# Softmax denominators inverted before a shared transpose, two steps of q on other engines, and a new order of an attention stage

## The chip, the core and the metric

One core of a Trainium2 chip runs the whole program. The metric is the time of one execution on the device in microseconds, from the first to the last work of the core. Its engines work side by side, each through its own list of instructions in order: TensorE (PE, matmuls and transposes), VectorE (DVE), ScalarE (ACT), GpSimd (POOL) and SyncE (SP, which here only issues DMA transfers). An instruction that waits for a semaphore holds everything behind it on its engine.

## What is computed

Three layers in a row: an attention with rotary positions, a feed-forward layer with a squared ReLU, and a layer of 8 experts of which each token takes one. The change lies in the first one.

```python
q_rot, k_rot = (rotate(q), rotate(k))                 # 4 batches, 8 heads, 576 positions, 64 wide
scores = scale * np.matmul(q_rot, k_rot.transpose(0, 1, 3, 2))
scores = scores - np.max(scores, axis=-1, keepdims=True)
attn = np.exp(scores)
attn = attn / (np.sum(attn, axis=-1, keepdims=True) + 1e-09)
attn_out = np.matmul(attn, v)                         # float32
x = attn_out.transpose(0, 2, 1, 3).reshape(2304, 512)
x = np.maximum(x @ w_in, 0.0) ** 2 @ w_out            # moe
return experts(x)                                     # moe2: gate, argmax, w1, relu, w2
```

## The kernel before

**Pairs.** The 32 heads are worked in 16 pairs, numbered 0 to 15. Each pair goes through steps that have short names; a name with a pair's number (pair 9's trm03) is one step of one pair. Numbers in float32 are kept as a high part in the form that PE reads (fp32r) and a low part, the remainder; a copy makes the high part, a subtraction the low one.

- ldk, ldq, ldv load k, q and v of a pair (SP). ak, bk, ck and aq, bq, cq turn k and q (two products with tables and a sum, L184, L186).
- kh0, kh1, kl0, kl1 split the two heads of k (copies L168 or L170, subtractions L173); kd0, kd1 copy the high part to the other 64 lanes. qh0, qh1, ql0, ql1 do the same for q: the digit is the head. vhi and vlo split v.
- sc0 to sc8 are nine tiles of scores (L238), 128 queries by 576 keys; sc8 holds the last 64 queries of both heads and takes twice the matmuls. mx0 to mx8 take the negated row maximum on DVE (L245), ex0 to ex8 the exponential on ACT (L256), which also sums each row into a column of a 128x9 tile.
- tr... transposes e on PE in tiles of 128x512 (L295): trm00 to trm13 for the main blocks (head, block), trrk and trrq for the remainders over keys and over queries, and trrr for the 64x64 corner of both remainders. eh... copies each to SBUF on ACT, el... subtracts the remainder on DVE (L173).
- srec adds 1e-9 to the sums and inverts them. In the kernel before it works on the transposed sums, 9 lanes of 128, in PSUM: trrr makes two transposes into one PSUM tile (L285, L286), ehrr and elrr read one half and srec (L265, L266) the other. rst stores the 9x128 result to memory; for block 0 (pairs 0 to 3) rld reads it back over 64 lanes and xn multiplies, later blocks are normalized in the next stage.
- pv00 to pv11 multiply with v (L329), p1.. copies the result to the tile xo (ACT), p2.. adds the two halves for pairs 0 to 3; xh and xl split the normalized result there, xr and xst store it.

**Rings.** Scores stand in a ring of two PSUM tiles, transposes and products in a ring of four called b, so a transpose waits until the tile four places back was read out. raw, vs, et0, et1, rk and xo have one buffer, the halves of q and k two, by the pair's parity; e and its sums have two tiles of the pool a_sb.

**Order.** The order is written out by hand as numbers: `FIRST`, `SECOND` and `PLAN` (from line 40) give each step a time and an engine (T for PE, A for ACT, V for DVE, P for POOL, D for a DMA on SP), for pair 0, pair 1 and all others; pair p is shifted by p x PERIOD (18), and all steps are recorded in the order of these numbers. The numbers only sort. So each engine's list interleaves two to four pairs. `TAIL` mixes in the first steps of the feed-forward layer: w.. steps convert int64 weights to float32 (wd loads one, wx on ACT, wy on DVE, wz on POOL, wb on DVE, wh on ACT, wl on POOL), xs0 to xs3 load the tokens of block 0, cl seven small constants, setup works on those, m10 to m12 are first products, re, sq, gg and gl the squared ReLU in two parts, m20 a second product. The unnamed step of the plan ("open") closes the pool a_prep, whose memory the feed-forward layer then takes.

Of the kernel before, what the change touches and what calls it, by code (L numbers as in the profile page):

```python
# [34 lines left out]
def f32(ap):  # L35
# [28 lines left out]
}  # L64
FIRST = {
# [25 lines left out]
}  # L91
SECOND = {
# [51 lines left out]
def attention(tc, qx, kx, v, tabq, tabk, ident, eye, xT, rD, ps, tail=None):  # L144
    nc = tc.nc
# [1093 lines left out]
```

## Time and profile before

| | us |
|---|---|
| median of 3 runs | 1060.05 (1059.29 to 1061.39) |
| the profiled execution | 1060.22 |
| its span, first to last instruction | 1058.4 |
| PE busy in the span | 942.7 |
| DVE | 740.3 |
| ACT | 543.3 |
| POOL | 391.7 |

Times in the views are microseconds from the span's start. The attention ends at 369 us with the last copy of pair 15; the conversion of the weights goes on to about 480 us, and from there TensorE works nearly without a gap. A row of a timeline gives the start, the duration, the engine, the line and the operation, the tile written and those read; in brackets stands how long the engine was idle before, and what ended that. A window gives each engine's busy time in a stretch and the clock that was granted to TensorE, as a share of 2.4 GHz: 0.5 is the lower level, 1.2 GHz.

### The profile page before, as it was taken

The page shows a single profiled execution, that of the slowest core. Times are in us where ns is not written, and L with a number is a line of the kernel's source. Part 1 is how long each engine was busy: PE and PEld are TensorE (multiplying, and loading weights), DVE is VectorE, ACT ScalarE, POOL GpSimd, SP SyncE. Part 2 cuts the span into 40 slices and gives each one's busy share as a digit, 9 for nine tenths or more (in the row PEclk, how much of TensorE's full clock was granted, in tenths as well). Part 3 has the DMA queues.
Part 4 walks back from the last instruction along what each step waited for, and adds up shares of the span by engine and source line. Part 5 has one row for each costly group of instructions (what it writes and reads, how often), then busy time and mean ns, then how long its engine had stood idle before and what let it go on. Part 6 is the DMA issues. An engine that isn't in the chain of part 4 may idle for free. (4 is left out here: it accounts for less than half of the span.)

```text
span 1058.4 us, 14903 instructions
## 1 busy us (share of the span) xinstructions
PE 942.7 (89%) x5194; PEld 817.8 (77%) x5194; DVE 740.3 (70%) x1298; ACT 543.3 (51%) x1089; POOL 391.7 (37%) x277
## 2 busy tenths in 40 slices
PE   2778888988988868878999999999999999999996
PEld 1667777887887846656887888788898889999995
DVE  5898878888888689997765575376456476566660
ACT  3677777887887746653223312321234325555551
POOL 7666676667664265564300220020001022212111
PEclk9899898999998989999999999999999999999998
DMA  6224344444443443543400310110015147766730
GB/s 235 92 87 138 116 121 145 130 139 134 129 137 81 129 141 120 170 138 131 155 5 1 119 41 1 60 41 1 1 41 180 40 159 222 237 214 224 241 121 31
DMA packets 50674, 122.90 MB, mean 116 GB/s; under 512 B 10960, under 2 KB 15584, under 8 KB 50592
## 3 DMA queue, kind: packets, MB, share of 16 engines
q1 hardware_dynamic: 47552, 112.17, 33.8%
q0 software_dynamic: 3040, 9.70, 2.6%
q8 instruction: 43, 0.70, 0.3%
q14 instruction: 39, 0.32, 0.1%
HBM read 98.23 MB, written 19.21 MB: 111 GB/s over the span
## 5 line engine op out<-in xcount | busy, mean ns | idle before, releaser
L658 PE MATMUL h<-xs,w 128*128 128x512 f32 (+1 forms) x720 | 169.6, 383 | 15.6 <-POOL w L511 15.6
L664 ACT ACTIVATE r<-h 128x512 f32<-128x512 f32 (+1 forms) x80 | 44.4, 555 | 237.5 <-PE h L658 194.8
L658 PEld LDWEIGHTS h<-xs,w 128*128 128x128 f32 x720 | 129.9, 194 | 46.9 <-POOL w L511 20.0
L672 DVE TENSOR_TENSOR g<-r 128x512 f32<-128x512 f32 (+1 forms) x80 | 65.1, 813 | 119.9 <-ACT r L664 119.1
L238 PE MATMUL sc<-kh,q 128*128 128x288 f32 x320 | 109.1, 356 | 40.4 <-DVE q L173 18.6
L295 PE MATMUL b<-ident,e 128*128 128x128 f32 x640 | 111.3, 316 | 34.5 <-DVE et L173 28.0
L693 PE MATMUL y<-w,gh 128*128 128x512 f32 x432 | 137.1, 399 | 0.0
L256 ACT ACTIVATE e<-sc,nmx 128x576 f32<-128x576 f32 x144 | 106.3, 740 | 50.2 <-DVE nmx L245 48.9
L245 DVE TENSOR_REDUCE nmx<-sc 128x1 f32<-128x576 f32 x144 | 105.7, 749 | 26.8 <-PE sc L238 25.5
L295 PEld LDWEIGHTS b<-ident,e 128*128 128x128 f32 x640 | 89.9, 163 | 43.8 <-DVE et L173 21.1
L238 PEld LDWEIGHTS sc<-kh,q 128*128 128x128 f32 x320 | 68.3, 214 | 50.4 <-issue 26.1
L930 DVE TENSOR_TENSOR w<-eraw,w 128x1024 fp32r<-128x1024 f32 x64 | 78.3, 1224 | 33.8 <-ACT w L929 33.7
L168 ACT ACTIVATE et<-b 128x512 fp32r<-128x512 f32 (+1 forms) x160 | 84.5, 550 | 25.4 <-PE b L295 24.7
L173 DVE TENSOR_TENSOR et<-b,et 128x512 fp32r<-128x512 f32 (+1 forms) x160 | 94.7, 623 | 4.0 <-ACT et L168 3.0
L238 PE MATMUL sc<-kl,q 128*128 128x288 f32 x320 | 96.9, 318 | 0.0
L693 PEld LDWEIGHTS y<-w,gh 128*128 128x128 f32 x432 | 81.3, 191 | 18.0
L693 PE MATMUL y<-w,gl 128*128 128x512 f32 x216 | 85.5, 396 | 0.0
L329 PE MATMUL b<-et,vs 128*128 128x288 f32 x512 | 80.7, 299 | 0.0
L975 PEld LDWEIGHTS h<-ye,w 128*128 128x128 f32 x576 | 75.1, 189 | 3.9
L975 PE MATMUL h<-ye,w 128*128 128x256 f32 x576 | 76.3, 283 | 0.0
L705 DVE SCALAR_TENSOR_TENSOR junk<-ysb,wgb 128x512 f32<-128x512 f32 x96 | 75.6, 841 | 0.0
L998 PE MATMUL y<-w,ge 128*128 128x512 f32 x288 | 75.3, 397 | 0.0
(218 smaller groups left out, 1836.5 us busy)
## 6 DMA issues: line engine op xcount, KB each, us to landing
eraw<-wexp SPq DMA_DIRECT2D x64, 512.0 KB, 3.6
wraw<-wio SPq DMA_DIRECT2D x32, 512.0 KB, 4.3
rawk<-kx SPq DMA_DIRECT2D x15, 640.0 KB, 3.9
rawq<-qx SPq DMA_DIRECT2D x15, 576.0 KB, 3.7
xT<-xo SPq DMA_DIRECT2D x24, 288.0 KB, 3.5
vraw<-v SPq DMA_DIRECT2D x16, 320.0 KB, 3.6
yD<-ysb SPq DMA_DIRECT2D x18, 256.0 KB, 2.0
kh<-kh SPq DMA_DIRECT2D x15, 160.0 KB, 2.4
```

Of the source, the lines that this page charges most:

```text
L168: nc.scalar.activation(out=out, in_=in_, func=ACTF.Copy)
L173: on[eng].tensor_tensor(out=out, in0=in0, in1=f32(hi), op=ALU.subtract)
L238: nc.tensor.matmul(out=sc(p, j)[:, half, 0:HS], lhsT=q[:, hd, q0:q0 + 128], rhs=k[:, hd, k0 + half * HS:k0 + half * HS + HS], start=(n == ...
L245: nc.vector.tensor_reduce(out=m, in_=sc(p, j)[:, :, 0:HS], axis=AX.XY, op=ALU.max, negate=True)
L256: nc.scalar.activation(out=e(p)[:, o:o + S].rearrange("p (a b) -> p a b", a=2), in_=sc(p, j)[:, :, 0:HS], func=ACTF.Exp, bias=live[p, f"nm ...
L295: nc.tensor.transpose(t[:, i * 128:(i + 1) * 128], x[:, o:o + 128], ident)
L329: nc.tensor.matmul(out=o, lhsT=lhsT.rearrange("p a b -> p (a b)"), rhs=rhs, start=(c == 0 and i == 0), stop=(c == 4 and i == 1))
L658: nc.tensor.matmul(out=h, lhsT=w[:, a, k * 128:(k + 1) * 128], rhs=xs[b, k][:, c], start=(k == 0 and i == 0), stop=(k == 3 and i == 2))
L693: nc.tensor.matmul(out=yp[t], lhsT=g[a][:, t * 128:(t + 1) * 128], rhs=w[:, c, 512:1024], start=(f == 0 and i == 0), stop=(f == NFC - 1 an ...
L705: nc.vector.scalar_tensor_tensor(out=junk, in0=ysb[j], scalar=1.0, in1=wgb[e], op0=ALU.mult, op1=ALU.mult, accum_out=lg[:, j, e:e + 1])
L930: nc.vector.tensor_tensor(out=w[:, 1], in0=r, in1=f32(w[:, 0]), op=ALU.subtract)
L975: nc.tensor.matmul(out=h, lhsT=w[:, a, k * 128:(k + 1) * 128], rhs=x[:, c], start=(k == 0 and i == 0), stop=(k == 3 and i == 2))
```

## The change

1. The sums lie behind e in the same tile (columns 9S to 9S+9, in 64 columns that are cleared once). e is no longer a tile of the pool a_sb, but one of two tiles of a_prep (e0, e1).
2. A new step sa adds 1e-9 to the 128x9 sums in place, on POOL. srec inverts them in place on DVE.
3. trrr is one transpose of the corner and the 64 columns behind it; the nine inverted sums come out in lanes 64 to 72 of the corner's tile. A new step sev copies them to rs on DVE.
4. In all pairs but pair 0, qh1 is ACT's and ql1 POOL's; both were DVE's. (Pair 0 keeps its engines.)
5. All four tables have new numbers.

```diff
 PLAN = {
-    "aq": (-96.168, "P"), ... "qh0": (-88.995, "V"), "qh1": (-88.827, "V"),
-    "ql0": (-87.629, "V"), ... "ql1": (-86.558, "V"), ...
+    "cq": (-76.464, "P"), "qh0": (-76.362, "V"), "qh1": (-74.157, "A"),
+    "ql0": (-73.664, "V"), "ql1": (-73.273, "P"), ...
+    ... "sa": (-45.720, "P"), ... "srec": (-44.605, "V"), ... "sev": (-42.856, "V"), ...
...
+        e_buf = [prep.tile([128, 9 * S + 64], F32, name=f"e{i}") for i in range(2)]
...
         def e(p):
-            return get(p, "e", [128, 9 * S], F32, 2)
+            return e_buf[p % 2]
 
         def sums(p):
-            return get(p, "sum", [128, 9], F32, 2)
+            return e(p)[:, 9 * S:9 * S + 9]
...
+        def guard(p, eng):
+            on[eng].tensor_scalar(out=sums(p), in0=sums(p), scalar1=1e-9, scalar2=None, op0=ALU.add)
+
         def srec(p, eng):
-            r = rs(p)
-            nc.vector.tensor_scalar(out=r, in0=tb(p, "rr")[0:9, 128:256], scalar1=1e-9, scalar2=None, op0=ALU.add)
-            nc.vector.reciprocal(out=r, in_=r)
+            nc.vector.reciprocal(out=sums(p), in_=sums(p))
+
+        def sev(p, eng):
+            copy(eng, rs(p), tb(p, "rr")[64:73, 0:128])
...
             if g == "rr":
-                nc.tensor.transpose(t[0:64, 0:128], x[:, 8 * S + 512:9 * S], ident)
-                nc.tensor.transpose(t[0:9, 128:256], sums(p), ident)
+                nc.tensor.transpose(t[:, 0:128], x[:, 8 * S + 512:9 * S + 64], ident)
                 return
...
+        for i in range(2):
+            nc.vector.memset(e_buf[i][:, 9 * S:9 * S + 64], 0.0)
```

The new numbers show in the engines' lists. Lines are those of each kernel. DVE, in the middle of the attention, around srec; et and rk are the transposed e, a number behind a name tells tiles apart; before:

```order
L173 TENSOR_TENSOR q_83<-rawq,q_83 64x576 x2
L173 TENSOR_TENSOR et_2465<-b,et_2465 128x512
L245 TENSOR_REDUCE nmx<-sc 128x1 x2
L265 TENSOR_SCALAR rs<-b 9x128
L266 RECIPROCAL rs<-rs 9x128
L173 TENSOR_TENSOR et_2465<-b,et_2465 128x512
L245 TENSOR_REDUCE nmx<-sc 128x1
L173 TENSOR_TENSOR et_2465<-b,et_2465 128x512
```

and now:

```order
L248 TENSOR_REDUCE nmx<-sc 128x1
L270 RECIPROCAL e_90<-e_90 128x9
L248 TENSOR_REDUCE nmx<-sc 128x1
L176 TENSOR_TENSOR et_2439<-b,et_2439 128x4x64
L176 TENSOR_TENSOR et_2514<-b,et_2514 128x4x64
L176 TENSOR_TENSOR rk<-b,rk 128x512
L173 COPY rs<-b 9x128
L248 TENSOR_REDUCE nmx<-sc 128x1
L176 TENSOR_TENSOR et_2439<-b,et_2439 128x512
L176 TENSOR_TENSOR rk<-b,rk 64x64 x2
L173 CAST q_84<-rawq 64x576
```

The two instructions of srec between the remainders (L265, L266) gave way to a short reciprocal between two maxima and a copy four rows on; one cast of q stands alone behind the remainders of the corner, with its subtraction further down.

POOL, one period; kl, vs and rawk, rawq are the low parts of k, v and the raw k and q, and L173 or L176 are subtractions; before:

```order
L186 TENSOR_TENSOR rawk<-rawk 128x640
L184 TENSOR_TENSOR rawq<-rawq,tabq 128x576 x2
L173 TENSOR_TENSOR kl_87<-rawk,kh_85 64x640
L173 TENSOR_TENSOR kl_87<-rawk,kh_85 64x576
L186 TENSOR_TENSOR rawq<-rawq 128x576
L173 TENSOR_TENSOR vs<-vraw,vs 128x10x64
L184 TENSOR_TENSOR rawk<-rawk,tabk 128x640 x2
L186 TENSOR_TENSOR rawk<-rawk 128x640
```

and now:

```order
L176 TENSOR_TENSOR q_83<-rawq,q_83 64x576
L187 TENSOR_TENSOR rawk<-rawk,tabk 128x640 x2
L189 TENSOR_TENSOR rawk<-rawk 128x640
L187 TENSOR_TENSOR rawq<-rawq,tabq 128x576
L267 TENSOR_SCALAR e_90<-e_90 128x9
L187 TENSOR_TENSOR rawq<-rawq,tabq 128x576
L176 TENSOR_TENSOR kl_88<-rawk,kh_86 64x640
L176 TENSOR_TENSOR kl_88<-rawk,kh_86 64x576
L189 TENSOR_TENSOR rawq<-rawq 128x576
L176 TENSOR_TENSOR vs<-vraw,vs 128x10x64
L176 TENSOR_TENSOR q_84<-rawq,q_84 64x576
```

The addition to the sums (L267) stands between the two products for q, the subtraction for v is followed by the one for q's second head, and only then does the next pair's k begin.

SP at the end of the attention; xT is the store of a pair's result, wraw the weights, c_, wg_sb, mb_sb and mod_sb the seven constants; before, where the four xs loads (L541) stand just ahead of the first row:

```order
L458 DMA wraw<-wio 128x512
L269 DMA rD<-rs 9x128
L356 DMA xT<-xo 64x2x576 x2
L600 DMA c_io_3901<-cst 128x8
L600 DMA c_io_3902<-cst 128x128
L600 DMA c_lt<-cst 128x128
L600 DMA c_id<-cst 128x18
L602 DMA wg_sb<-wg 128x4x8
L603 DMA mb_sb<-mb 128x16
L604 DMA mod_sb<-mod 128x18x2
L356 DMA xT<-xo 64x2x576 x2
L458 DMA wraw<-wio 128x512 x13
```

and now, from the xs loads on:

```order
L549 DMA xs<-xT 128x2x512 x4
L362 DMA xT<-xo 64x2x576 x2
L276 DMA rD<-rs 9x128
L362 DMA xT<-xo 64x2x576 x2
L608 DMA c_io_3872<-cst 128x8
L608 DMA c_io_3873<-cst 128x128
L608 DMA c_lt<-cst 128x128
L608 DMA c_id<-cst 128x18
L610 DMA wg_sb<-wg 128x4x8
L611 DMA mb_sb<-mb 128x16
L612 DMA mod_sb<-mod 128x18x2
L466 DMA wraw<-wio 128x512 x14
```

The constants stood ahead of the last xT stores and stand behind them now, with all further weights behind the constants. The xs loads stand ahead of the stores of pairs 14 and 15 in both; they go into memory that a_prep gave up, in which e0 and e1 lie now, and did not before.

## Rows read from the trace of the kernel before

**Rows 1.** Windows: busy us of PE, PEld, DVE, ACT, POOL; granted clock; DMA share, GB/s.
```profile
235.50:255.65 20.15, 17.68 (x124) 16.79 (x124) 16.33 (x29) 15.89 (x39) 13.21 (x10) 0.92 0.44 124
239.10:242.60 3.50, 1.46 (x11) 1.26 (x12) 3.46 (x7) 1.54 (x5) 3.42 (x3) 0.99 0.37 92
242.60:246.00 3.40, 3.40 (x18) 3.37 (x17) 3.37 (x7) 2.74 (x7) 1.81 (x2) 0.51 0.39 114
400.00:460.00 60.00, 49.68 (x188) 37.77 (x186) 58.43 (x69) 36.89 (x62) 36.97 (x24) 0.91 0.46 154
```

**Rows 2.** Timeline of POOL: start, us, what, idle before and releaser; vlo, and kl1.
```profile
38.17 1.63 POOL L173 TENSOR_TENSOR vs<-vraw,vs 128x640 fp32r<-128x640 f32 x1
...
85.85 1.84 POOL L173 TENSOR_TENSOR vs<-vraw,vs 128x640 fp32r<-128x640 f32 x1 [2.35 <-ACT vs L168]
...
175.14 1.56 POOL L173 TENSOR_TENSOR vs<-vraw,vs 128x640 fp32r<-128x640 f32 x1 [3.77 <-ACT vs L168]
...
235.50 1.55 POOL L173 TENSOR_TENSOR vs<-vraw,vs 128x640 fp32r<-128x640 f32 x1 [4.03 <-ACT vs L168]
...
246.46 1.57 POOL L173 TENSOR_TENSOR kl<-rawk,kh 64x640 fp32r<-64x640 f32 x1 [2.05 <-ACT kh L168]
...
334.77 1.57 POOL L173 TENSOR_TENSOR vs<-vraw,vs 128x640 fp32r<-128x640 f32 x1 [2.52 <-ACT vs L168]
```

**Rows 3.** Timeline of DVE: q of pair 1, then of pair 11, then srec.
```profile
36.25 2.16 DVE L170 CAST q<-rawq 64x576 fp32r<-64x576 f32 x2
...
39.11 3.07 DVE L173 TENSOR_TENSOR q<-rawq,q 64x576 fp32r<-64x576 f32 x2
...
252.43 0.93 DVE L170 CAST q<-rawq 64x576 fp32r<-64x576 f32 x2
253.39 1.54 DVE L173 TENSOR_TENSOR q<-rawq,q 64x576 fp32r<-64x576 f32 x2
...
258.75 0.28 DVE L265 TENSOR_SCALAR rs<-b 9x128 f32<-9x128 f32 x1 [1.66 <-ACT rk L168]
259.06 0.94 DVE L266 RECIPROCAL rs<-rs 9x128 f32<-9x128 f32 x1
```

**Rows 4.** Timeline of ACT: a cast of q in pair 0; an exponential.
```profile
14.68 0.68 ACT L168 ACTIVATE q<-rawq 64x576 fp32r<-64x576 f32 x1
...
241.09 0.74 ACT L256 ACTIVATE e<-sc,nmx 128x576 f32<-128x576 f32 x1 [1.91 <-DVE nmx L245]
```

**Rows 5.** Timeline of PE: transposes in a period and in the drain; second product.
```profile
240.44 0.66 PE L295 MATMUL b<-ident,e 128*128 128x128 f32 x4 [1.36 <-DVE et L173]
...
359.01 4.26 PE L295 MATMUL b<-ident,e 128*128 128x128 f32 x24 [2.56 <-DVE et L173]
...
384.86 1.22 PE L693 MATMUL y<-wf,gh 128*128 128x512 f32 x2 [7.63 <-ACT gh L668]
```

**Rows 6.** Groups of POOL, whole span: count, busy us and mean ns, idle before.
```profile
L885 POOL TENSOR_TENSOR rhs<-rhs,val 128x306 fp32r<-128x306 f32 x3 | 2.6, 884 | 47.9 <-DVE rhs L879 47.8
...
L173 POOL TENSOR_TENSOR q<-rawq,q 64x576 fp32r<-64x576 f32 x1 | 1.4, 1411 | 0.8 <-ACT q L168 0.8
...
L1216 POOL MEMSET const-uint8-127<- 128x1 uint8 x1 | 0.1, 119 | 0.0
```

**Rows 7.** Timeline of SP, the DMA queue, at the attention's end.
```profile
360.08 1.92 SPq L600 DMA_DIRECT2D c_io<-cst  x2
...
364.02 0.43 SPq L604 DMA_DIRECT2D mod_sb<-mod  x1
369.32 1.23 SPq L356 DMA_DIRECT2D xT<-xo  x2
370.65 47.98 SPq L458 DMA_DIRECT2D wraw<-wio  x12
```

**Rows 8.** DMA issues: count, KB each, median us from issue to landing.
```profile
wraw<-wio SPq DMA_DIRECT2D x32, 512.0 KB, 4.3
...
xT<-xo SPq DMA_DIRECT2D x24, 288.0 KB, 3.5
```

More of the change, by code (lines that the diff above doesn't have):

```diff
@@ L373, in xst @@
             nc.sync.dma_start(out=xT[p, :, :, 0:N0], in_=f32(xh(p)))
-        fs = dict(ldv=ldv, vhi=vhi, vlo=vlo, srec=srec, rst=rst, rld=rld, xr=xr, xn=xn, xh=xhi, xl=xlo, xst=xst)
+        fs = dict(ldv=ldv, vhi=vhi, vlo=vlo, sa=guard, srec=srec, sev=sev, rst=rst, rld=rld, xr=xr, xn=xn, xh=xhi, xl=xlo, xst=xst)
         for x in "qk":
```

190 rows, old and new, of tables (FIRST, PLAN, SECOND, TAIL) are left out of this document.

## Prediction

> **What bounds the kernel now.** I read the windows first. The attention runs to 369 us [rows 7]; behind it comes a stage in which DVE is busy 58.43 of 60 us, and then one filled by TensorE [rows 1]. All edits lie in the attention, or at its end. There no engine is full: in one period of 20.15 us PE is busy 17.68, DVE 16.33, ACT 15.89, POOL 13.21 [rows 1]. So the order binds, and the question is which waits make the loop.
>
> The start of vlo on POOL, one a pair, gives the pace: pairs 6 to 14 stand 159.63 us apart, 19.95 a pair; pairs 2 to 6, with extra work for block 0, 89.29, or 22.3; pairs 0 to 2, 47.7 [rows 2]. Within a period the loop is this. DVE comes to srec and waits 1.66 us, because L265 reads the PSUM tile that ACT is copying out of (ehrr); then it spends 0.28 and 0.94 on it [rows 3]. The maxima and remainders behind it come late: ACT idles 1.91 us for mx2 [rows 4] and PE 1.36 us for a tile of ring b [rows 5]. PE, busy 1.46 of 3.5 us there, then works at a granted clock of 0.51, the lower level, in the next 3.4 us [rows 1].
>
> **The change part by part.** *Denominators.* Out of DVE's queue go L265 (0.28) and the long reciprocal (0.94), and with them the wait of 1.66 [rows 3]. In come a reciprocal of 9 elements a lane and sev, a copy of the 9x128 shape of L265, so 0.28. The reciprocal took 0.94 for 128 elements a lane; for 9 it lies between nothing and 0.94, and I take 0.15, by element count. It waits for sa, the addition of 1e-9 on POOL. POOL's nearest rows are 0.12 us (one element a lane) and 0.88 (306) [rows 6]; I take 0.2, since 9 is near 1. One transpose less on PE is under 0.3 us in PE's slack. The wait does not vanish by itself: sev must wait for the shared transpose, and srec for sa; both are rivals below. In the order PE makes that transpose right behind sc1, and DVE has mx2, elrq and elrk (some 2 us) between srec and sev, which covers it.
>
> *q's second head.* qh1 goes from DVE (half of 0.93) to ACT (0.68 for the same shape in the first pair), ql1 from DVE (half of 1.54) to POOL (1.41) [rows 3, 4, 6]. Loads of a period then are: DVE 16.33 - 0.46 - 0.77 - 1.22 + 0.15 + 0.28 = 14.3; ACT 15.89 + 0.68 = 16.6; POOL 13.21 + 1.41 + 0.2 = 14.8. ACT is now the fullest, so a period is at least 16.6.
>
> *What remains of q on DVE.* Before, both casts and both subtractions stood where POOL idles (it waits 4.03 us for vhi), and cost 0.93 and 1.54. In the first pairs, with POOL at work, the same two pairs of instructions took 2.16 and 3.07 [rows 2, 3]. In the new order qh0 follows elrr, about a microsecond after vhi, when POOL has begun vlo; ql0 comes two maxima later, when POOL runs ql1. So each meets a POOL instruction. One cast costs 0 to 1.2 more, one subtraction 0 to 0.8; I take 0.5 (vlo is half done) and 0.7. Behind them stand mx8 and mx4, for which ACT waits, and ACT has no spare time: 1.2 us a period on the path. The Trainium skill says of this, in "GPSIMD Engine Reference", section Specifications, that GpSimd's SBUF interface is shared with VectorE and contended by DVE instructions with two SBUF inputs or in a two-port mode. By that rule taken in full it would be the rival B; the longer rows of the first pairs agree with it.
>
> *The order.* Period forecast: 16.6 + 1.2 + 0.2 for waits that I can't place (ACT idles 4.26 a period now) = 18.0, between 17.2 and 18.6. In a timetable by hand PE's thinnest stretch of 3.4 us holds four groups of transposes and a double score tile, about 2.5 us of work against 1.46 now, so I expect the granted clock to stay at the upper level. POOL: ak and aq wait for loads that start when kl0 and ql1 are done and land 4 us later; POOL has cq, vlo and ql1, or ak, bk and ck (over 4 us), in between, so no wait there.
>
> *The sum.* Nine steady periods (the eight of [rows 2] and the one with pair 15's scores): 9 x (19.95 - 18.0) = 17.6 less. Pairs 2 to 6: they stay 2.35 above a steady period, plus 0.45 because xn and xl meet a fuller POOL, so 20.8: 4 x 1.5 = 6 less (2 to 10). Front: half of the contended 2.16 and 3.07 goes from in front of pair 1's scores: 3 less (from 7 less to 2 more). Drain of pair 15: PE's 2.56 us wait behind srec stands uncovered [rows 5], and the transposes after it run slow: 3 less (1 to 4).
>
> *The handover costs.* Two things get worse at the attention's end. First, the seven loads of constants, 4.4 us of SP's time, ran beside the last transposes; they now stand behind the last xT store, and all weight loads from wd7 on behind them [rows 7]. Today the next weight load is issued at 370.65, right behind that store, and PE's second product starts at 384.86, 15.5 us behind the end of p110 [rows 5]. wd7 will be issued 1.3 + 4.4 behind it and land 4.3 later [rows 8]; wx7 then runs 4 us later than now. Second, e is now a tile of the pool that closes early, so the xs tiles of the next stage lie in its memory: their loads must wait for the last transpose of pair 15. The store of pair 14 stands behind them on SP, and p100 of pair 15 needs xo back from it: three issues, 1.3 us for the store, 3.5 to land [rows 8]; the p1 copies end some 3 us later. Together 7 more, between 2.5 (if DVE's own chain covers most of it) and 10.
>
> -17.6 - 6 - 3 - 3 + 7 = -22.6. The profiled execution took 1060.22 (span 1058.4), beside a median of 1060.05, so no correction: 1037.6, say 1038. The ends of the period and of the handover give 1024 to 1048.
>
> **The rivals.** *B, contention in full.* qh0 and ql0 wait out whole POOL instructions, 1.2 and 0.8, and POOL is held in turn: period 19.1. Then 9 x 0.85 = 7.7, and 2, 1 and 2 for pairs 2 to 6, front and drain, against 7: 6 less, 1054. For it: the rows of the first pairs [rows 3]. Against: POOL has 3 us of idle time a period in which they may fall. *C, sev takes the place of the wait.* If PE is late, DVE waits for the shared transpose as it did for ehrr; only the 0.94 is saved, and contention takes 1.2 of it back. Period 19.9 or so, drain and front 4 less, handover 4 to 7 more: 1060. Against: PE has more slack in the new order. *A, slower: sa holds DVE.* POOL works in order. If its waits stay as long as now (4.03 for vhi, 2.05 for kh [rows 2]), a POOL period is 14.8 + 6.1 = 20.9, plus the wait of sa for the last exponential, 0.5: 21.4 against 19.95. DVE stands at srec until sa is done, and all maxima behind it: 13 periods x 1.4 = 18 more, and 7 for the handover: 1085. It decides from 5.2 us of POOL waits a period (20.0 - 14.8); above that the kernel is slower. For it: POOL gets the two new steps and is in DVE's path for the first time. Against: vlo now has ql1 and the k of the next pair behind it, and the new places of kh0 and vhi on ACT match its order.
>
> **How the numbers follow.** Forecast 0.58, B 0.17, C 0.09, A 0.16. About 0.2% (2 us) is what a measurement can tell from no change. Faster: forecast and B, 0.75; same: C, 0.09; slower: A, 0.16. The range has to leave out no more than 0.2: it takes in the forecast's ends, B and C, up to 1063, and leaves A and a little below 1024.
>
> **What would show it.** Right: vlo starts 17.2 to 18.6 apart in pairs 6 to 14; DVE's wait ahead of sev and srec under 0.3 each; ACT busy over 90% of a period; the granted clock at the upper level in steady periods; qh0 about 0.9 and ql0 about 1.4; the second product 20 to 25 us behind the last p110. Wrong: the reciprocal waiting for POOL by more than 1 us (A), sev waiting for PE by as much (C), a clock that still falls once a period, or an early part that is longer than 47.7 and 89.3.

## The result, and the profile after

The changed kernel takes 1032.34 us (median of four runs, 1031.78 to 1033.71), the kernel before in the same comparison 1060.72: the ratio is 0.973, with a 95% interval of 0.970 to 0.976. The forecast was 1038 (1024 to 1063). The profiled execution of the changed kernel took 1031.78, with a span of 1030.0. So 28.4 us went out of the span, where 22.6 were forecast.

The windows of the changed kernel (start and end, length, then busy us of PE, PEld, DVE, ACT and POOL, the granted clock, DMA share and GB/s), first over pairs 6 to 14, then over one period; they answer to [rows 1]; the third row is the kernel before over the same pairs:

```profile
165.40:305.60 140.20, 133.26 (x972) 121.98 (x971) 123.73 (x209) 128.21 (x312) 112.46 (x82) 1.00 0.49 141
218.26:235.78 17.52, 16.65 (x123) 15.21 (x123) 15.44 (x27) 16.15 (x40) 15.41 (x11) 1.00 0.51 143
175.14:334.77 159.63, 139.79 (x974) 131.95 (x974) 132.92 (x226) 126.99 (x305) 107.04 (x73) 0.93 0.44 128
```

A period is 140.05/8 = 17.51 us, and the granted clock is 1.00 all through these eight, the upper level; before it was 0.93 over the same pairs, and fell to 0.51 in the period shown in [rows 1]. Now every engine is nearly full, and PE is the fullest: of 17.52 us PE is busy 16.65, ACT 16.15, DVE 15.44, POOL 15.41.

POOL's timeline (start, us, what, idle time before and its releaser): vlo of pairs 0, 2, 6, 9 and 14, as in [rows 2], and what follows it in pair 9's period:

```profile
38.38 1.95 POOL L176 TENSOR_TENSOR vs<-vraw,vs 128x640 fp32r<-128x640 f32 x1
...
93.64 1.55 POOL L176 TENSOR_TENSOR vs<-vraw,vs 128x640 fp32r<-128x640 f32 x1
...
165.71 1.55 POOL L176 TENSOR_TENSOR vs<-vraw,vs 128x640 fp32r<-128x640 f32 x1
...
218.29 1.55 POOL L176 TENSOR_TENSOR vs<-vraw,vs 128x640 fp32r<-128x640 f32 x1
220.69 1.42 POOL L176 TENSOR_TENSOR q<-rawq,q 64x576 fp32r<-64x576 f32 x1 [0.85 <-ACT q L171]
222.20 1.95 POOL L187 TENSOR_TENSOR rawk<-rawk,tabk 128x640 f32<-128x640 f32 x1
...
305.76 1.55 POOL L176 TENSOR_TENSOR vs<-vraw,vs 128x640 fp32r<-128x640 f32 x1 [4.53 <-ACT vs L171]
```

DVE's, one period, as in [rows 3]: qh0, ql0, srec (L270), mx2, and sev (L173 COPY):

```profile
219.36 0.79 DVE L173 CAST q<-rawq 64x576 fp32r<-64x576 f32 x1
...
221.45 1.28 DVE L176 TENSOR_TENSOR q<-rawq,q 64x576 fp32r<-64x576 f32 x1
...
231.49 0.20 DVE L270 RECIPROCAL e<-e 128x9 f32<-128x9 f32 x1
232.73 0.76 DVE L248 TENSOR_REDUCE nmx<-sc 128x1 f32<-128x576 f32 x1 [1.04 <-PE sc L241]
...
234.83 0.28 DVE L173 COPY rs<-b 9x128 f32<-9x128 f32 x1
```

ACT's: qh1, ex8, ex4 (with its accumulator read) and ex6 of that period, as in [rows 4]; ehrr (behind sev, which DVE starts at 234.83); then the last four p1 copies and the first step of wx7:

```profile
219.87 0.68 ACT L171 ACTIVATE q<-rawq 64x576 fp32r<-64x576 f32 x1
...
221.45 0.74 ACT L259 ACTIVATE e<-sc,nmx 128x576 f32<-128x576 f32 x1 [0.28 <-DVE nmx L248]
...
224.15 0.74 ACT L259 ACTIVATE e<-sc,nmx 128x576 f32<-128x576 f32 x1 [0.89 <-DVE nmx L248]
224.79 0.19 ACT L259 ACTIVATION_READ_ACCUMULATOR e<-sc,nmx 128x1 f32 x1
224.88 0.73 ACT L259 ACTIVATE e<-sc,nmx 128x576 f32<-128x576 f32 x1
...
235.57 0.45 ACT L171 ACTIVATE rk<-b 64x64 fp32r<-64x64 f32 x2
...
331.54 1.32 ACT L171 ACTIVATE xo<-b 128x288 f32<-128x288 f32 x4 [9.24 <-DMA xT<-xo]
...
343.81 0.66 ACT L489 ACTIVATE wmag<-wraw 128x512 f32<-128x512 f32 x1 [7.68 <-DMA wraw<-wio]
```

srec takes 0.20 and sev 0.28, and neither waits. qh0 takes 0.79 and ql0 1.28, since POOL is at work beside them. In this period ACT waits only for mx8 and mx4, the two maxima around ql0.

The rest is the attention's end. PE's timeline (pv00 in mid-attention, then m10 and m20, as in [rows 5]):

```profile
220.90 1.29 PE L335 MATMUL b<-et,vs 128*128 128x288 f32 x8 [0.17 <-DVE et L176]
...
332.00 8.11 PE L666 MATMUL h<-xs,wf 128*128 128x512 f32 x26 [5.24 <-ACT xo L171]
...
354.68 1.22 PE L701 MATMUL y<-wf,gh 128*128 128x512 f32 x2 [11.46 <-ACT gh L676]
```

SP's (xs, the stores of pairs 14 and 15, constants, weights), as in [rows 7]:

```profile
307.76 15.32 SPq L549 DMA_DIRECT2D xs<-xT  x4
323.18 1.26 SPq L362 DMA_DIRECT2D xT<-xo  x2
...
332.88 1.23 SPq L362 DMA_DIRECT2D xT<-xo  x2
334.16 1.85 SPq L608 DMA_DIRECT2D c_io<-cst  x2
...
338.58 3.35 SPq L466 DMA_DIRECT2D wraw<-wio  x4
```

The xs loads occupy SP for 15.32 us, in which they wait for pair 15's last transposes. Before, they held SP for 11.31 us too, but from 341.41, and were done at 352.7, ahead of pair 14's last copy, so no store waited behind them. Now, behind them, at 323.18, the store of pair 14 goes out, and p100 of pair 15 has waited 9.24 us for it when it starts at 331.54. The constants follow the last store, the next weights go out at 338.58, and wx7 waits 7.68 for the first of them. Both waits stop DVE as well, which stands 5.48 us at wy5 and 3.36 at wy7.

### The profile page after: what moved, and what is told of

It reads as the page before. It is cut to its first block, busy times and chain, and to the rows that moved or that the text cites. A ratio compares the mean times of both kernels' runs of the same rounds, so it can differ in the third digit from the quotient of the medians.

```text
span 1030.0 us, 14885 instructions
## 1 busy us (share of the span) xinstructions
PE 926.9 (90%) x5178; PEld 796.6 (77%) x5178; DVE 717.6 (70%) x1270; ACT 548.5 (53%) x1104; POOL 416.9 (40%) x308
## 5 line engine op out<-in xcount | busy, mean ns | idle before, releaser
L680 DVE TENSOR_TENSOR g<-r 128x512 f32<-128x512 f32 (+1 forms) x80 | 67.3, 842 | 125.0 <-ACT r L672 124.3
L241 PE MATMUL sc<-kh,q 128*128 128x288 f32 x320 | 104.4, 342 | 29.4 <-ACT kh L171 15.8
L301 PE MATMUL b<-ident,e 128*128 128x128 f32 x640 | 91.9, 280 | 12.6 <-DVE et L176 5.2
L176 DVE TENSOR_TENSOR et<-b,et 128x512 fp32r<-128x512 f32 (+1 forms) x160 | 97.2, 628 | 4.2 <-ACT et L171 3.4
L241 PEld LDWEIGHTS sc<-kh,q 128*128 128x128 f32 x320 | 63.0, 197 | 40.1 <-issue 16.4
L241 PE MATMUL sc<-kl,q 128*128 128x288 f32 x320 | 92.5, 304 | 1.1 <-DVE kl L176 1.1
L301 PEld LDWEIGHTS b<-ident,e 128*128 128x128 f32 x640 | 76.0, 144 | 19.9 <-PE b L292 6.6
L335 PEld LDWEIGHTS b<-et,vs 128*128 128x128 f32 x512 | 70.6, 188 | 14.2 <-issue 7.5
L585 POOL TENSOR_TENSOR xraw<-xraw,rbs 128x512 f32<-128x512 f32 (+1 forms) x12 | 15.4, 1283 | 162.2 <-DMA rbs<-xT 162.0
L1013 POOL DMA_INDIRECT out<-ob,six x19 | 20.5, 1078 | 142.2 <-ACT ob L1012 111.8
```

What stands on the lines that cost most here:

```text
L176: on[eng].tensor_tensor(out=out, in0=in0, in1=f32(hi), op=ALU.subtract)
L241: nc.tensor.matmul(out=sc(p, j)[:, half, 0:HS], lhsT=q[:, hd, q0:q0 + 128], rhs=k[:, hd, k0 + half * HS:k0 + half * HS + HS], start=(n == ...
L301: nc.tensor.transpose(t[:, i * 128:(i + 1) * 128], x[:, o:o + 128], ident)
L335: nc.tensor.matmul(out=o, lhsT=lhsT.rearrange("p a b -> p (a b)"), rhs=rhs, start=(c == 0 and i == 0), stop=(c == 4 and i == 1))
L680: nc.vector.tensor_tensor(out=g, in0=rs[n], in1=rs[n], op=ALU.mult)
```

## The experiments

### Three parts, in every combination

The change has three parts: the form of the denominators, the move of q's second head, and the order. Each was tried with and without the others. The short edits:

```diff
 # denominators alone, in the old order (PLAN; FIRST and SECOND likewise)
+    "sa": (-69.4, "P"), "srec": (-66.6, "V"), "sev": (-64.047, "V"),     # srec: reciprocal of the 128x9 sums
-    "srec": (-64.047, "V"),
-                nc.tensor.transpose(t[0:9, 128:256], sums(p), ident)     # one transpose, as in the change
```

```diff
 # denominators back, in the new order: sev does what srec did
         def sev(p, eng):
-            copy(eng, rs(p), tb(p, "rr")[64:73, 0:128])
+            r = rs(p)
+            nc.vector.tensor_scalar(out=r, in0=tb(p, "rr")[0:9, 128:256], scalar1=1e-9, ...)
+            nc.vector.reciprocal(out=r, in_=r)
```

```diff
 # q back, in the new order (PLAN and SECOND); q alone, in the old order, is the reverse
-    "qh1": (-74.157, "A"), "ql1": (-73.273, "P"),
+    "qh1": (-74.157, "V"), "ql1": (-73.273, "V"),
```

In the old order e lies in the pool that stays open, so the handover is the old one there; in the new order e lies in a_prep, so "order" below takes in the handover with its cost. What was expected:

Denominators alone, old order: 

> The kernel before with the denominators part alone (sa on POOL behind cq, srec ahead of trrr, sev where srec stood; e in the pool that stays open, so the handover is as before). Theory 1, the wait ahead of srec and the long reciprocal make the loop: DVE loses 1.66 + 1.22 and gains 0.20 + 0.28 a pair, so the steady period falls from 19.95 to 18.5 or less, all in all 14 x 1.4 = 20 less, 1040. Theory 2, the order makes the loop and the wait only moves to sev or to the maxima: period 19.5 or more, 1053 to 1062.

The new order alone: 

> The new order with the old denominators (two transposes, L265 and L266 at sev's place) and both heads of q back on DVE. Theory 1: the long reciprocal and both casts and subtractions are on DVE again (0.94 + 0.28 - 0.48 + 0.7 + 1.3, or 2.7 a pair on top of a 15.4 load), so the period is 19 or more and, with the handover that the new order makes worse, the time is 1050 to 1065. Theory 2, the order is what counts: period below 18, time below 1042.

The change without its denominators: 

> The changed kernel with the old denominators alone put back (L265, L266 at sev's place, two transposes, no sa). Theory 1: 0.74 more work on DVE and a wait for the corner's copy, part of it in DVE's 1.9 us of idle time a period: period 18.2 to 19.0, 1042 to 1054. Theory 2, the order has room for the old form: period under 17.8, under 1036.

The change without q's move: 

> The changed kernel with q's second head back on DVE in all pairs (the same numbers, only the engines). Theory 1: DVE gets 0.7 and 1.3 more a period and has 1.9 idle in pieces, ACT loses 0.68 and POOL 1.42, so DVE binds: period 18.2 to 19, 1042 to 1054. Theory 2, ACT binds the period: it falls with ACT's load, 17.5 to 17.0, and the time is 1024 to 1032.

q's move alone, old order: 

> The kernel before with the move of q's second head alone (qh1 on ACT, ql1 on POOL, the same numbers). Theory 1, the loop runs through all that DVE does: 1.2 us less DVE work a pair shortens the period by 0.6 to 1.0, from 19.95 to 19.2, time 1046 to 1052. Theory 2, the wait for the corner's copy alone sets the period and swallows what is saved ahead of it: 19.7 or more, 1056 to 1063.

Denominators and q, old order: 

> The kernel before with both the denominators part (as in the run with that alone, whose period was 18.80) and the move of q's second head, in the old order and with the old handover. Theory 1, the order itself is worth little: the two parts add up, period 17.6 to 18.0, time 1026 to 1031. Theory 2, the new order is what makes room for them: period 18.4 or more, time 1035 to 1040.

Measured (vlo of pairs 0 to 2 in us; pairs 2 to 6 and 6 to 14 in us a pair):

| order | denominators | q | us | ratio, 95% | 0 to 2 | 2 to 6 | 6 to 14 |
|---|---|---|---|---|---|---|---|
| old | old | old | 1060.7 | | 47.7 | 22.32 | 19.95 |
| old | new | old | 1039.9 | 0.980 (0.976 to 0.983) | 39.7 | 21.13 | 18.80 |
| old | old | new | 1056.0 | 0.994 (0.992 to 0.996) | 41.1 | 21.43 | 20.18 |
| old | new | new | 1037.1 | 0.977 (0.974 to 0.980) | 42.2 | 20.00 | 18.96 |
| new | old | old | 1073.5 | 1.011 (1.007 to 1.016) | 65.6 | 20.96 | 20.15 |
| new | new | old | 1061.6 | 1.001 (0.999 to 1.004) | 62.8 | 20.52 | 18.85 |
| new | old | new | 1035.6 | 0.976 (0.972 to 0.979) | 57.4 | 18.00 | 17.57 |
| new | new | new | 1032.3 | 0.973 (0.970 to 0.976) | 55.3 | 18.02 | 17.51 |

Against these expectations: the denominators alone came to theory 1's time, with a period of 18.80 where 18.5 or less was expected. The order alone and the change without q's move came to theory 1's periods (20.15 and 18.85), but both some 8 us above its times, since their early pairs are slow as well. The other three came out by theory 2: the change without its denominators (17.57), q's move alone (20.18), and denominators and q in the old order (18.96).

No part has a worth of its own. The denominators are worth 21 and 19 us in the old order (without and with q's move), 12 and 3 in the new one; the 3 are within the scatter. q's move gives 3 to 5 in the old order, where the period even grows by 0.2, and 29 to 38 in the new one. The order costs 13 by itself (vlo of pair 14 starts at 348.26 there and at 334.77 before, so the loss lies in the pairs and not in the handover) and gives 5 on top of both parts, 13 once its handover is mended (below). So 21 of the 28 us can be had in the old order from the denominators alone; in the new one 25 of them come from q's move and the order together.

**Where the wait belongs.** The prediction tied DVE's 1.66 us ahead of L265 to the form. In the old order with the new form DVE's timeline reads (srec, then sev):

```profile
221.81 0.20 DVE L274 RECIPROCAL e<-e 128x9 f32<-128x9 f32 x1
...
224.32 0.28 DVE L177 COPY rs<-b 9x128 f32<-9x128 f32 x1 [1.67 <-ACT rk L175]
```

and ACT's, for ehrr:

```profile
223.85 0.44 ACT L175 ACTIVATE rk<-b 64x64 fp32r<-64x64 f32 x2
```

sev waits 1.67 us for the same copy of the corner that L265 waited for; the transpose itself had ended at 222.46. What fell is the work: 0.28 and 0.94 became 0.20 and 0.28, with 0.28 alone left behind the wait, and the period lost 1.15. That is more than the 0.94 that went from there; the granted clock rose too, from 0.93 to 0.97 over pairs 6 to 14, and the two were not separated. In the new order with the old form, L265 and L266 (here L274, L275) follow their neighbours on DVE with no wait at all:

```profile
218.73 0.27 DVE L274 TENSOR_SCALAR rs<-b 9x128 f32<-9x128 f32 x1
219.03 0.94 DVE L275 RECIPROCAL rs<-rs 9x128 f32<-9x128 f32 x1
```

So the wait belongs to the place. The table of before has srec behind ehrr (-64.047 against -64.916), and the second reader of the PSUM tile waited for the first. The new table has sev ahead of ehrr (-42.856 against -41.788), and there ehrr runs behind it (235.57 against 234.83). No run moved srec alone ahead of ehrr in the old order; what that would have given by itself is not shown.

**What q holds.** With q's second head back on DVE in the new order, the window over pairs 6 to 14 reads:

```profile
183.00:333.80 150.80, 133.42 (x970) 121.81 (x969) 134.32 (x225) 121.87 (x303) 104.78 (x74) 1.00 0.45 131
```

and ACT's timeline has ex8 and ex4 of one period as:

```profile
224.63 0.74 ACT L259 ACTIVATE e<-sc,nmx 128x576 f32<-128x576 f32 x1 [1.72 <-DVE nmx L248]
...
228.12 0.74 ACT L259 ACTIVATE e<-sc,nmx 128x576 f32<-128x576 f32 x1 [1.69 <-DVE nmx L248]
```

DVE is busy 134.32/8 = 16.8 of 18.85 us a pair, and ACT waits 1.72 and 1.69 for the maxima mx8 and mx4, where it waited 0.28 and 0.89: mx8 stands behind both casts of q, mx4 behind all four steps. Theory 1 held for the period, theory 2 (ACT binds) fell.

**What the clock does not do.** Windows of the order alone, pairs 6 to 14:

```profile
187.10:348.30 161.20, 135.35 (x978) 123.73 (x977) 142.82 (x225) 122.48 (x303) 102.37 (x66) 0.99 0.41 122
```

The granted clock is 0.99 there, at the upper level nearly throughout, and the period is 20.15, longer than before with its fall in each period (0.93 over pairs 6 to 14 before). So a steady upper level is not enough to make the kernel fast. What part the clock has in the gain of the changed kernel is not shown: no run has its order with the lower level in it.

### The handover mended

```diff
-        e_buf = [prep.tile([128, 9 * S + 64], F32, name=f"e{i}") for i in range(2)]
+        e_buf = [sb.tile([128, 9 * S + 64], F32, name=f"e{i}", bufs=1) for i in range(2)]
...
-    "xs0": (-64.359, "D"), ... "wz3": (-29.679, "P"), "wb3": (6.702, "V"), "wd7": (144.662, "D"), "cl": (-35.359, "D"),
+    "xs0": (-59.8, "D"), ... "wz3": (-47.2, "P"), "wb3": (-47.1, "V"), "wd7": (-47.0, "D"), "cl": (-46.0, "D"),
```

The second form has `"cl": (300.0, "D")`, so that wd8 goes out behind the last store and ahead of the constants.

> The changed kernel with the handover mended: e0 and e1 in the pool that stays open, the xs loads behind the store of pair 14, the load wd7 behind them (with wz3 and wb3, which it waits for, ahead of the corner of TAIL) and the constants ahead of pair 15's store. Theory 1, the wait of p100 for the store of pair 14 (9.2 us on ACT) and that of wx7 for its load (7.7) lengthen the path: the last copy of the attention ends 327 instead of 332.9, the first product of the second kind (m20) begins 344 to 347 instead of 354.7, time 1021 to 1026. Theory 2, the weight steps on DVE bind behind the attention in any case: m20 moves, the time stays within 1029 to 1033.

> The kernel with the handover mended, with the load wd8 also ahead, behind the last xT store, and the constants between wd8 and wd9. In the run before this one wx8 waited 6.5 us for its load, issued at 332.6 behind constants and store, and DVE 3.05 of it. Theory 1: wd8 goes out at 328 and m20 starts 3 us earlier, at 344; time 1020 to 1023. Theory 2, the constants come late now and setup waits for them instead: within 1 us of 1024.3.

Measured: 1024.30 us (ratio 0.964, 0.961 to 0.967), and 1023.94 (0.963, 0.959 to 0.966) in the second form. ACT's timeline in the first form (p100, then wx8):

```profile
322.75 0.41 ACT L171 ACTIVATE xo<-b 128x288 f32<-128x288 f32 x1 [0.58 <-ACT et L171]
...
339.62 0.66 ACT L489 ACTIVATE wmag<-wraw 128x512 f32<-128x512 f32 x1 [6.51 <-DMA wraw<-wio]
```

PE's (m10, m20):

```profile
326.49 6.24 PE L666 MATMUL h<-xs,wf 128*128 128x512 f32 x26
...
347.30 1.22 PE L701 MATMUL y<-wf,gh 128*128 128x512 f32 x2 [8.96 <-ACT gh L676]
```

SP's (the store of pair 14, xs, wd7, the later weights):

```profile
316.76 1.23 SPq L362 DMA_DIRECT2D xT<-xo  x2
318.04 3.22 SPq L549 DMA_DIRECT2D xs<-xT  x4
...
324.92 0.34 SPq L466 DMA_DIRECT2D wraw<-wio  x1
...
332.60 12.05 SPq L466 DMA_DIRECT2D wraw<-wio  x5
```

p100 starts at 322.75 instead of 331.54 and the last p1 copy ends 5.8 us earlier; m10 no longer waits; m20 starts 7.4 earlier, and the span is 7.2 shorter. Theory 1 held: what the handover delays is paid to the end, though DVE is busy 19 of each 20 us from 360 to 440 behind it. In the second form wx8 no longer waits for its load (it starts at 336.70), but the next weight step waits 3.29 us for its own, and m20 starts at 346.96 where theory 1 had 344. The 0.4 us can't be told from nothing, as theory 2 had it; that setup binds in its place is not shown.

### The steps of q against POOL

Three tries at the remaining waits, each two numbers of PLAN or a few more instructions:

```diff
 # ql0 early, elm13 late
-    "ql0": (-73.664, "V"), "mx8": (-56.110, "V"),
+    "ql0": (-76.0, "V"), "mx8": (-57.0, "V"),
 # qh0 and ql0 behind elm13; the last run has these numbers for pairs 7 to 15 only, on the mended handover (second form)
-    "qh0": (-76.362, "V"), "ql0": (-73.664, "V"),
+    "qh0": (-74.5, "V"), "ql0": (-74.3, "V"),
 # sa five times as long
-            on[eng].tensor_scalar(out=sums(p), in0=sums(p), scalar1=1e-9, ...)
+            for i in range(5):
+                on[eng].tensor_scalar(out=sums(p), in0=sums(p), scalar1=0.0 if i else 1e-9, ...)
```

> The changed kernel with ql0 right behind qh0, where POOL waits 0.85 us for qh1, and mx8 ahead of elm13 (two numbers of PLAN). Theory 1, ql0 took 1.28 because POOL worked beside it, and lies on the path to the exponentials: ql0 takes 0.75 to 0.8, the period falls from 17.51 to 17.0 to 17.2, time 1025 to 1029. Theory 2, ACT and PE's ring of score tiles set the period: 17.4 to 17.6, 1030 to 1034, with ql0 as short.

Measured: 1051.85 us (ratio 0.990), pairs 6 to 14 18.10 a pair, pairs 2 to 6 21.1. Both theories fell. DVE's timeline (qh0, ql0, elm13 with elm12, mx6):

```profile
219.17 0.79 DVE L173 CAST q<-rawq 64x576 fp32r<-64x576 f32 x1
219.99 0.75 DVE L176 TENSOR_TENSOR q<-rawq,q 64x576 fp32r<-64x576 f32 x1
...
221.45 1.28 DVE L176 TENSOR_TENSOR et<-b,et 128x512 fp32r<-128x512 f32 x2
...
224.40 0.76 DVE L248 TENSOR_REDUCE nmx<-sc 128x1 f32<-128x576 f32 x1 [1.01 <-PE sc L241]
```

PE's (pv00):

```profile
222.28 1.29 PE L335 MATMUL b<-et,vs 128*128 128x288 f32 x8 [1.74 <-POOL q L176]
```

ql0 takes 0.75, as hoped. But pv00 takes the tile of ring b that elm13 frees, and elm13 now stands behind ql0 and mx8: its first half ends at 221.45 + 0.68 = 222.13, and pv00 starts at 222.28 after 1.74 us, against 0.17 in the changed kernel. The profile names POOL's ql1, which ended at 222.19; but in the changed kernel pv00 starts at 220.90 while ql1 runs (220.69 to 222.11), so it can't be that. With pv00 late, sc6 is late, and mx6 waits 1.01. More than half of the loss, 12 us, lies in pairs 2 to 6, which this period does not explain.

> The changed kernel with qh0 and ql0 both behind elm13 instead of around it and mx8 (two numbers of PLAN). Unlike the run with ql0 early and elm13 late, elm13 comes earlier here, so the tile of ring b that pv00 takes is free in time. Theory 1, DVE's casts and subtractions of q beside POOL are on the path: qh0 falls behind vlo and takes 0.46 instead of 0.79, ql0 0.75 to 1.0 instead of 1.28, ACT's waits for mx8 and mx4 go from 1.17 to 0.8 a period: 17.0 to 17.3, 1026 to 1030. Theory 2, the time that DVE saves turns into waits for PE's score tiles: 17.4 to 17.7, 1030 to 1035.

Measured: 1038.86 us (ratio 0.976, 0.971 to 0.980; 1033.23 to 1039.61): slower than the changed kernel in the median, but with a period of 17.24 in pairs 6 to 14, as theory 1 had it. DVE's timeline shows ql0 of an early pair, then both steps in a steady one:

```profile
119.23 1.90 DVE L176 TENSOR_TENSOR q<-rawq,q 64x576 fp32r<-64x576 f32 x1
...
228.79 0.44 DVE L173 CAST q<-rawq 64x576 fp32r<-64x576 f32 x1
229.26 0.75 DVE L176 TENSOR_TENSOR q<-rawq,q 64x576 fp32r<-64x576 f32 x1
```

In the steady pair neither step is made longer by POOL, and over pairs 6 to 14 ACT's waits for maxima fall from 10.1 us to 7.4, or from 1.26 to 0.93 a pair. So by this run, of the 0.34 and 0.53 that POOL adds to qh0 and ql0 in the changed kernel, 0.27 a period are on the path.

The loss is in pairs 2 to 6, 19.83 a pair against 18.02, and in pairs 0 to 2, 57.7 against 55.3. In three of the four pairs from 2 to 6 ql0 meets ql1 (119.09 to 120.51 on POOL in the pair shown) and takes 1.88 to 2.03, where it takes 0.75 in the changed kernel; qh0 takes 0.65 to 0.68 there instead of 1.41 to 1.56. The two together are as long as before, so which wait makes the loss is open. Hence the last run:

> The kernel with the handover mended (second form), and qh0 and ql0 both behind elm13 in pairs 7 to 15 alone. With that order in all pairs the steady period was 17.24, but the early pairs lost 6 us, all in all 1038.9. Theory 1, the loss belongs to the early pairs, whose extra steps for block 0 shift what meets what: pairs 6 to 14 17.25 a pair, pairs 0 to 6 as in the changed kernel, 2 us less than the mended handover alone, 1020 to 1023. Theory 2, the order costs at any place (the pairs that follow must find their rhythm again): period 17.5 or more, 1024 to 1034.

Measured: 1022.37 us (ratio 0.963, 0.960 to 0.965), pairs 2 to 6 18.04, pairs 6 to 14 17.24. The pace of the pairs bears out theory 1. The time, the lowest of all, is 1.6 below the mended handover alone, which is within the scatter: pairs 0 to 2, with the same numbers in both, took 56.8 there and 57.7 here.

> The changed kernel with the step sa five times as long (four more additions of zero on POOL, 0.96 us more a pair). The prediction's slower rival in small: POOL holds DVE at srec. Theory 1: DVE comes to srec 1.8 us behind sa's end and POOL has 1.6 us of waits a period left, so the period stays within 0.3 of 17.51 and the time within 1031 to 1037. Rival: POOL is full in effect and the period grows by all of the 0.96: 18.4, time 1044 to 1048.

Measured: 1043.45 us (ratio 0.982); pairs 0 to 2 57.9, 2 to 6 19.38, 6 to 14 17.90 a pair. POOL's timeline (the five additions, vlo):

```profile
222.64 1.54 POOL L268 TENSOR_SCALAR e<-e 128x9 f32<-128x9 f32 x5 [0.78 <-ACT e L259]
...
230.04 1.55 POOL L176 TENSOR_TENSOR vs<-vraw,vs 128x640 fp32r<-128x640 f32 x1
```

DVE's (qh0, ql0):

```profile
230.12 1.79 DVE L173 CAST q<-rawq 64x576 fp32r<-64x576 f32 x1
...
233.20 0.75 DVE L176 TENSOR_TENSOR q<-rawq,q 64x576 fp32r<-64x576 f32 x1
```

srec still doesn't wait for sa. But POOL comes to vlo later, qh0 now meets all of it and takes 1.79 instead of 0.79, ACT waits 1.32 for mx8 instead of 0.28, and ql0 in turn is not held. Of 0.96 us more work on POOL (the five take 1.54 with what lies between them, the one 0.24) 0.39 reach the steady period, and 8 of the 11 us are lost in the early pairs. The time is near the rival's, the period between the two theories, and neither's mechanism is it: POOL acts on DVE through q's steps, not through sa.

## Why the prediction held, and where it did not

The sum, by the prediction's own marks (vlo of pairs 0, 6 and 14, the last xT store at 369.32 and 332.88, m20, the end):

| stretch | forecast | measured |
|---|---|---|
| to vlo of pair 0 | 0 | +0.2 |
| pairs 0 to 6 | -3 - 6 = -9 | +7.6 - 17.2 = -9.6 |
| pairs 6 to 14 | 8 x -1.95 = -15.6 | -19.6 |
| pair 14 to the last store | -1.95 - 3 + 3 = -2 | -7.4 |
| last store to m20 | +4 | +6.3 |
| m20 to the end | 0 | +1.8 |
| sum | -22.6 | -28.4 |

- **The period** was forecast at 18.0 and is 17.51, and the three terms of its sum, 16.6 + 1.2 + 0.2, were each off: they came near in part because the errors offset each other. *ACT's work* was 16.6 and measured 128.21/8 = 16.03. The move itself was sized rightly: with q's move alone in the old order ACT is busy 132.41/8 = 16.55 a pair over pairs 6 to 14, 0.68 more than the 126.99/8 = 15.87 before. But the new order takes 0.64 off ACT's busy time: with q back on DVE it is 121.87/8 = 15.23. ACT's instructions, added one by one, take some 18.5 us a pair before and 18.7 there, so it is their overlap that grew: where one stands right behind another it starts some 0.1 us before that one ends (ex6 at 224.88, the read ahead of it ends at 224.98). The Trainium skill has this in "ScalarE: Activation LUTs", section What ACT_TABLE_LOAD costs: back-to-back ACTIVATE instructions overlap by about 93 ns; these rows agree. *The contention* was forecast at 0.5 + 0.7, all of it on the path; it measured 0.34 + 0.53, of which 0.27 were on the path, by the run with both q steps behind elm13. *The waits without a place* were put at 0.2 and make up the rest, 17.51 - 16.03 - 0.27 = 1.2. So "ACT is now the fullest" fell too: PE is, with 16.65 of 17.52 us.
- **Contention**, in kind: right, and rival B (whole instructions waited out) is what happens when POOL runs later, as the run with the longer sa shows.
- **The denominators**: the chain was read rightly for the old order, where they alone give 21 us. The step that failed is "and with them the wait of 1.66": the wait stays in the old order (1.67 ahead of sev) and is absent in the new one with either form, so the new form is worth only 3 us there, within the scatter. Rival C's mechanism, sev waiting in srec's place, is real in the old order, and even there the shorter form came with 1.15 less a period.
- **The clock** stayed at the upper level in the steady periods, as forecast; the run with the order alone shows that this is not enough for a gain.
- **Pairs 0 to 6**: right in sum, wrong in parts. By the prediction's own words an early part longer than 47.7 speaks against it, and 55.3 is; vlo stands further back in a pair's work now, which moves time between the two stretches. That the excess of pairs 2 to 6 over a steady one stays at 2.35 was wrong: it is 0.51. In the four pairs of kernels in the table that differ in q's move alone, the excess is smaller with it (2.37 to 1.25, 2.33 to 1.04, 1.67 to 0.51, 0.81 to 0.43), so part of it was DVE's load. The rest is open.
- **The end of the attention**: the drain was sized too small. Without the handover's wait (5.8 us, by the mended kernel) this stretch would be 13 shorter and not 5. vlo of pair 15 follows that of pair 14 by 13.5 us now, and by 20.7 before; why was not taken apart.
- **The handover**: both mechanisms were named and are there. 7 us were forecast; the mended kernel gets back 8.
- **Rival A** (POOL holds DVE at srec) didn't come: the waits of POOL that it counted on, 4.03 for vhi and 2.05 for kh, are gone, and 0.85 (for qh1) and 0.78 (for the last exponential, ahead of sa) a period are left. Its price list was right in one point: POOL has almost nothing to spare, and 0.96 us more cost 11.

So the direction and the handover were right for the reasons given. The total is nearer than its parts: the steady periods and the drain were too cautious by 9 us and the rest too kind by some 4. Which part carries the gain was not seen: in the new order q's move does, with 29 to 38 us, and the denominators add some 3 on top; in the old order it is the other way round, 19 to 21 for the denominators and 3 to 5 for q.

## What to carry to other kernels

When work is moved off an engine and the order is redone with it, cost the parts together: here the order alone loses 13 us, q's move alone gives 5, and the two together 25. Ask of a wait whether it belongs to the instruction or to its place in the list; here the second reader, put ahead of the first, did as well in its old form (17.57 against 17.51 a pair). And when a stage's memory is handed on, look at what is queued behind the loads that now wait: another pool and a few numbers gave 8 us.

## What the runs showed of the hardware

A DVE instruction on q from SBUF to SBUF that meets a running POOL instruction waits until that one ends. In the changed kernel qh0 ends at 220.15, 0.31 behind vlo's end at 219.84, and ql0 at 222.73, 0.62 behind ql1's end at 222.11; with the longer sa qh0 ends at 231.91, 0.32 behind vlo's at 231.59. Alone they take 0.44 and 0.75. So the price of a cast is not a factor but follows what is left of POOL's instruction, 0.34 or 1.35 here. POOL pays too: the product that starts at 222.20, under ql0, takes 1.95, where one that meets nothing takes some 1.55. Maxima and remainders, which read PSUM, ran beside POOL at their usual 0.75 and 0.68. The Trainium skill says, in "SBUF — State Buffer", section SBUF: two separate sides, that GpSimd and DVE share a pair of ports, that a GpSimd instruction and a DVE instruction that has two SBUF inputs or is in a two-port mode lock it against each other, and that the one that starts first holds it for its whole length; these rows agree.
